# A fused attention and mixture-of-experts kernel: the tokens of experts three to eight turned by DMA transposes in place of TensorE transposes

## The chip, the cores and the metric

The kernel runs on one core of a Trainium2 chip. Its time is the device time of one execution in microseconds (us). The engines of a core work side by side, each in the order of its own queue: PE (TensorE, matmuls and transposes; PEld is its weight load), DVE (VectorE), ACT (ScalarE), POOL (GpSimd) and SP (SyncE, which here issues most DMAs). They wait for each other by semaphores.

## The reference

Attention over 8 batches of 12 heads, 448 positions and head size 64, with capped scores, is followed by a layer of eight experts to which tokens are given greedily.

```python
scores = cap * tanh(scale * q @ k.T / cap)
attn   = exp(scores - max); attn /= sum + 1e-9
x      = (attn @ v) as 3584 tokens x 768
logits = x @ w_gate                      # 8 experts, cap = 448 tokens each
for idx in argsort(-logits.flatten()):   # best (token, expert) pair first
    if token is free and expert has room: assign
for e in range(8):
    h = maximum(x[mask] @ w1[e], 0)      # 768 -> 1024
    out[mask] = h @ w2[e]                # 1024 -> 768
```

All is float32. Every expert gets exactly 448 tokens.

## The kernel before, in words

**Stages.** `attention` takes some 335 us and writes x (token by token) to a DRAM tensor `xs`. `ffn_all` first finishes what attention left over, with the search for the first expert's tokens between, and then runs the eight experts. The experts are found one after another: the search finds which expert fills first and which 448 tokens it gets, the FFN of that expert runs, and the search for the next one runs in the gaps.

**The order of the work.** In `ffn_all` PE, ACT, DVE and POOL run in the order in which the source writes their instructions (`manual_schedule`, L701). SP is not in that list; its DMAs are placed by the scheduler. The FFN is a sequence of matmuls; after each one `tick` (L806) counts up `now`. The search is a Python generator (`phases0`, L669, with `select`, `search` and `finalise`); every `yield n` means "go on n ticks later", and `step` (L690) then writes its next few instructions into the queues between two FFN matmuls. So the search's steps stand at fixed places between matmuls. In one step of `select` some compares are put on DVE (L503) and, for thresholds from the third on, on ACT (L500, `cmpA`); some ticks later PE adds their counts up (L507, `psR`), and DVE derives the next thresholds (L511, L515). The last step of `finalise` is a PE matmul (L644) and a DVE reduction (L648) that give `idx`, the token list. Then come the update of the search's tables (L651 on), 9 ticks, the proposals of the next search, 30 ticks, and `search`, whose first compares come 5 ticks later. For the eighth expert `last` (L590) stands in place of the search; it has no compares.

**One expert.** A period is 320 ticks. `ffn1` (L814) runs for f = 0 to 7: 18 matmuls each, 128 features of the 1024, for 448 tokens, as three products per slice of 128 of the 768 columns. `ffn2` (L846) runs for u = 0 to 7: four blocks of tokens (128, 128, 128, 64) times two halves of 384 output columns, 24 matmuls each, 16 for the last block. Float32 operands are cut into a rounded part and a rest ("h" and "l"), on ACT and on POOL for weights (`cut`, L752: `w1h`, `w1l`, `w2h`, `w2l`), on ACT and DVE for x (`cutx`, L800: `xgh`, `xgl`). PSUM tiles `psH` (three buffers) are emptied by ACT (L833, L861, L864).

**The tokens.** When `idx` is known, the next `tick` calls `gather` (L777): four indirect DMAs from POOL bring the 448 rows of 768 floats into the tile `xgp`, tokens on partitions, 128, 128, 128 and 64. The FFN needs x with columns on partitions. `xtr(p,c)` (L792) turns one slice of 128 columns: four PE transposes into a PSUM tile `psX`, then `cutx`. For experts three to eight, the list `CP` (L771) puts the six calls into `ffn2` of the expert before: u = 5 after matmuls 12 and 20, u = 6 after 4 and 20, u = 7 after 4 and 12. For the first two experts other lists say where, and these stay.

**The weights.** `load1` (L738) brings one eighth of w1 (384 KB), `load2` (L745) a quarter of w2 (768 KB), both from SP, with four buffers each. The source calls those of the next expert at u = 4 (w1 0 and 1), 5 (w1 2, w2 0), 6 (w1 3) and 7 (w2 1); SP can issue one as soon as it has read the expert's number and a buffer is free, since nothing ties it to PE's place.

Of the kernel before, what the change touches and what calls it, by code (L numbers as in the profile page):

```python
# [6 lines left out]
F32=mybir.dt.float32; F32R=mybir.dt.float32r; BF16=mybir.dt.bfloat16; F16=mybir.dt.float16; I32=mybir.dt.int32; I16=mybir.dt.int16  # L7
AF=mybir.ActivationFunctionType; ALU=mybir.AluOpType; AX=mybir.AxisListType
# [323 lines left out]
class Routing:  # L332
# [266 lines left out]
    def finalise(s,wp,L,update):  # L599
# [49 lines left out]
        s.results.append((idx,s.ei))  # L649
        yield 1  # L650
        if update:  # L651
          with s.tc.issue_after(mark.ins) if s.cur==0 else nullcontext():
            z=wp.tile([112,1],F32,name="zz")
            v.tensor_scalar(z,oi[:,0,0,0:1],0.0,None,op0=ALU.mult)
            v.scalar_tensor_tensor(gt,m[:,0,:],z,m[:,1,:],op0=ALU.add,op1=ALU.add)
            v.scalar_tensor_tensor(qq,pi,s.cap-0.5,gt,op0=ALU.is_lt,op1=ALU.mult)
            v.scalar_tensor_tensor(T["op"],qq,-2.0,T["op"],op0=ALU.mult,op1=ALU.add)
            ns=wp.tile([112,8],F32,name="ns"); pen=wp.tile([112,8],F32,name="pen")
            v.tensor_scalar(ns,s.e8c,s.e8s,z,op0=ALU.not_equal,op1=ALU.add)
            v.tensor_scalar(pen,ns,-0.5,2.0,op0=ALU.add,op1=ALU.mult)  # L660
            v.tensor_scalar(pen,pen,FMAX,None,op0=ALU.mult)
            v.tensor_tensor(s.e8m,s.e8m,ns,op=ALU.mult)
            v.tensor_tensor(L,L,pen.unsqueeze(1).broadcast_to([112,NC,8]),op=ALU.min)
            yield 9
# [15 lines left out]


W1B=4; W2B=4
def ffn_all(nc, tc, ctx, rt, xs, w1, w2, out, ident, E, wp, deferred, xctx, gen):
# [11 lines left out]
    def units(n):  # L695
        for _ in range(n):
            if deferred: late.append(deferred.pop(0)())
    def posts():
        while late: late.pop(0)()
    N0=1; UN=[1,2,1,2,0,2,2,1,2,2,0,2,2,2,0,0]  # L700
    ctx.enter_context(tc.manual_schedule(engines={ET.PE,ET.Activation,ET.DVE,ET.Pool}))  # L701
    with tc.issue_after(rt.mark[0].ins):
        units(1)
    posts()
    m=0
    wu=[None]; end=[-99]
# [31 lines left out]
    def load1(p,i,gate=None):  # L738
        if p>=E: return
        e=expert(p)  # L740
        t=ws.tile([128,DC,128],F32,name="w1r",bufs=W1B)
        if gate is not None: nc.gpsimd.tensor_copy(t[0:1,0,0:1],gate)
        nc.sync.dma_start(t,w1[bass.ds(e,1),:,i*128:i*128+128].rearrange("o (c p) f -> p (o c) f",p=128))
        raw[p,1,i]=t
# [23 lines left out]
        view=use=lambda t:t.rearrange("p (o d) -> p o d",o=2)  # L768
        cut((p,2,hf,i),src,[128,2*HD],"w2",8,None,view,use)
    xgs={}; xgT={}  # L770
    CP=[[int(y) if y!='-' else None for y in x] for x in ',,,,,-01,2-3,45'.split(',')]  # L771
    CL=[[]]*6+[[None,None,0],[1,2]]
    def newx(p):
        if p not in xgT: xgT[p]=(fp.tile([128,DC,C],F32R,name="xgh"),fp.tile([128,DC,C],F32R,name="xgl"))
# [2 lines left out]
    def gather(p):  # L777
        if p>=E or p in xgs: return
        need(p)
        t=xgs[p]=xgp  # L780
        for j,(o,n) in enumerate(TS):
            g=nc.gpsimd.indirect_dma_start(out=t[:n,j*DM:(j+1)*DM],out_offset=None,in_=xs,in_offset=bass.IndirectOffsetOnAxis(ap=res[p][0][:n,j:j+1],axis=0))  # L782
        return g
# [8 lines left out]
    def xtr(p,c):  # L792
        if p>=E or c is None: return
        newx(p)
        gather(p)
        ps=pt.tile([128,512],F32,name="psX")
        for j,(o,n) in enumerate(TS):
            nc.tensor.transpose(ps[:,o:o+128],xgs[p][:,j*DM+c*128:j*DM+c*128+128],ident)  # L798
        cutx(p,c,ps)
    def cutx(p,c,ps):  # L800
        h,l=xgT[p]
        src=ps[:,:C]
        nc.scalar.activation(h[:,c,:],src,AF.Copy)  # L803
        lo=nc.vector.tensor_tensor(l[:,c,:],src,h[:,c,:].bitcast(F32),op=ALU.subtract)
    pend=[]; cnt=[0]; cur=[0]; bc=[0]; BG=11
    def tick(n=1):  # L806
        cnt[0]+=n; bc[0]+=n; now[0]+=n
        if bc[0]>=BG:
            if pend: bc[0]=0; scatter(*pend.pop(0))
        if len(res)>cur[0]+1 and cur[0]+1 not in xgs: bc[0]=0; gather(cur[0]+1)  # L810
        if cnt[0]>=hint[0]:
            cnt[0]=0; step()
    hh={}
# [52 lines left out]
    need(0)  # L866
    WG=3; NW=12; WJ=4
    for i in range(WG): load1(0,i)
    mk=gather(0)
    with tc.issue_after(mk.ins):  # L870
        tok=xgp[0:1,2*DM:2*DM+1]
        for i in range(WG,W1B): load1(0,i,tok)
        load2(0,0,tok)
        load2(0,1,tok)
    warm(NW)
    step(); step()
    step()
# [5 lines left out]
    for p in range(E):  # L883
        lastp=p==E-1; cur[0]=p
        for f in range(FC):
            if f==0: load2(p,2)
            if f+W1B-1<FC and (p==0 or f+W1B-1>=W1B): load1(p,f+W1B-1) if (p,1,f+W1B-1) not in raw else None
            if f==2: load2(p,3)
            work={}
            if f+2<FC and (p,1,f+2) not in spl: work[3]=[lambda: split1(p,f+2)]  # L890
            at={0:[(11,0,0)],1:[(11,0,1)],2:[(11,0,2)],3:[(11,1,0)],4:[(11,0,3)],5:[(11,1,1)],6:[(11,1,2)],7:[(11,1,3)]}
            if p==0: at={1:[(11,0,0)],2:[(11,0,1)],3:[(11,0,2)],4:[(11,0,3)],5:[(11,1,0)],6:[(3,1,1),(11,1,2)],7:[(3,1,3)]}
            for n,hf,i in at.get(f,()): work[n]=[lambda hf=hf,i=i: split2(p,hf,i)]
            if p==1 and f==0: work[1]=[lambda: xtr(1,4)]; work[4]=[lambda: xtr(1,5)]
            ffn1(p,f,work)
        if lastp:
            while pend: scatter(*pend.pop(0))
            ih=f2.tile([128,2],I32,name="ih")
            for k in range(2): nc.gpsimd.tensor_scalar(ih[:,k:k+1],res[p][0][:,2:3],2.0,float(k),op0=ALU.mult,op1=ALU.add)
            nc.gpsimd.drain()  # L900
            lp[0]=False
            out2=out.rearrange("n (q d) -> (n q) d",q=2)
            for t,hf in [(t,hf) for t in (3,0,1,2) for hf in range(2)]:
                ffn2(p,t,hf,[])
                if t==2: put(out2,ih[:,hf:hf+1],ons[p][0][:,t*DM+hf*HD:t*DM+hf*HD+HD])
                elif hf==1: scatter(p,t)
            break
        for u in range(8):
            if u==4: load1(p+1,0); load1(p+1,1)
            if u==5: load1(p+1,2); load2(p+1,0)  # L910
            if u==6: load1(p+1,3)
            if u==7: load2(p+1,1)
            wk={5:{14:[lambda: split1(p+1,0)]},6:{8:[lambda: split1(p+1,1)]}}.get(u,{})
            if p<1 and u==7: wk={15:[lambda: xtr(1,3)]}
            ffn2(p,u%4,u//4,(CL if p<1 else CP)[u],wk)
            if u>3: pend.append((p,u%4))


def full(nc,tc,q,k,v,cap,wg,w1,w2,out):
    with ExitStack() as ctx:  # L920
# [2 lines left out]
        xs=dr.tile([3584,768],F32,name="xs")  # L923
        NDEF=4
        xd=dr.tile([2 if NDEF<4 else NDEF-2,128,6,448],F32,name="xd")
        ident=cp.tile([128,128],F32,name="ident"); make_identity(nc,ident)
        L1=cp.tile([112,32,8],F32,name="L1")
        r=Routing(nc,cp,3584,8); r.ident=ident; r.tc=tc
# [18 lines left out]
        ffn_all(nc,tc,ctx,r,xs,w1,w2,out,ident,8,wp,deferred,xctx,r.phases(wp,L1,turned))  # L947


_INS=["q","k","v","cap","moe_w_gate","moe_w1","moe_w2"]  # L950
# [24 lines left out]
```

## Time and profile before

| | |
|---|---|
| median of 3 runs | 906.31 us (905.91 to 907.29) |
| the profiled execution | 906.85 us, its span 905.1 us |
| mean granted PE clock | 0.995 |
| PE busy | 876.5 us, 97% of the span |
| PE transposes of `xtr` (L798) | 176, mean 272 ns |
| `gather` DMAs (L782) | 32, mean 1.07 us on POOL |
| DMA queue q1 (SP's DMAs) | 285104 packets, 99.70 MB |

The profile shows one execution. A timeline row gives the start in us from the span's start, the duration, the engine, the source line, the operation, the tile written and the tiles read, the shape, a count, and in brackets how long the engine sat idle before it and which instruction ended that. A row of groups gives busy us, mean ns, and idle time before. A row of a windows view gives, for a stretch of time, each engine's busy us, then the granted PE clock (1.00 is full), the share of the DMA engines and GB/s. Matmuls are pipelined: a row's duration overlaps the next one's start, so the distance of starts counts.

### The profile page before, as it was taken

How to read it: one execution, taken by the hardware profiler on the slowest of the kernel's cores; microseconds unless marked ns; L12 is line 12 of the kernel's file. 1: busy time of each engine (PE TensorE's matmuls, PEld its weight loads, DVE VectorE, ACT ScalarE, POOL GpSimd, SP SyncE). 2: the span in 40 equal slices, each digit the busy share in tenths (PEclk: the TensorE clock that was granted, in tenths of full speed). 3: DMA queues.
4: the chain of work that ended last, by engine and by line, in shares of the span. 5: the costliest groups of instructions: out<-in, count | busy, mean ns of one | idle time of the engine just before them, and what ended most of it. 6: DMA issues, size and time to landing. Idle time of an engine off the chain costs nothing.

```text
span 905.1 us, 17559 instructions
## 1 busy us (share of the span) xinstructions
PE 876.5 (97%) x6320; PEld 643.3 (71%) x6320; DVE 604.0 (67%) x2004; ACT 564.0 (62%) x844; POOL 349.9 (39%) x501
## 2 busy tenths in 40 slices
PE   6899999999999997799999999999999999999997
PEld 3333444444333345789989989989999999999997
DVE  3688988989888888766776776767767764231210
ACT  6998898889899948273582672762752752532521
POOL 8100000000000009482593492592682773754841
PEclk9999999999999999999999999999999999999999
DMA  8799999997994017741915616407407407416301
GB/s 117 113 136 140 128 171 173 139 164 120 198 175 72 1 58 246 248 157 45 313 45 171 196 36 226 157 19 236 150 18 253 149 3 251 149 55 236 112 10 53
DMA packets 291704, 123.09 MB, mean 136 GB/s; under 512 B 224768, under 2 KB 275712, under 8 KB 291104
## 3 DMA queue, kind: packets, MB, share of 16 engines
q1 hardware_dynamic: 285104, 99.70, 49.9%
q0 software_dynamic: 4656, 22.02, 6.8%
q8 instruction: 50, 0.82, 0.4%
q10 hardware_dynamic: 1856, 0.23, 0.2%
q14 instruction: 38, 0.31, 0.1%
HBM read 97.15 MB, written 24.77 MB: 135 GB/s over the span
## 4 chain that ended last, share of the span: by engine, by line
PE 72%; issue 12%; POOL 5%; DVE 5%; SPq 3%; DMA 1%; ACT 1%; POOLq 0%; ACTq 0%; DVEq 0%
PE psH L827 20%; PE psH L855 18%; PE psA L189 12%; PE psS L148 10%; PE psM L206 4%; SPq L92 2%; PE psS L153 2%; POOL w1l L759 2%; PE psX L798 2%; PE psM L37 1%; POOL out_dram L840 1%; POOL w2l L759 1%; DVE es L165 1%; POOL xg L782 1%; DVE cmpD L503 1%
## 5 line engine op out<-in xcount | busy, mean ns | idle before, releaser
L855 PE MATMUL psH<-w2h,hh 128*128 128x384 f32 x896 | 247.0, 342 | 0.0
L855 PE MATMUL psH<-w2l,hh 128*128 128x384 f32 x512 | 175.0, 342 | 0.0
L154 ACT ACTIVATE e<-psS 128x896 f32<-128x896 f32 x168 | 147.6, 909 | 31.3 <-PE psS L148 18.7
L855 PEld LDWEIGHTS psH<-w2h,hh 128*128 128x128 f32 x896 | 162.3, 189 | 0.2
L159 ACT ACTIVATE e<-e,bias 128x1792 f32<-128x1792 f32 (+2 forms) x74 | 147.3, 1991 | 2.0
L827 PE MATMUL psH<-xgh,w1h 128*128 128x448 f32 x384 | 143.4, 373 | 0.3 <-ACT xgh L803 0.3
L827 PE MATMUL psH<-xgh,w1l 128*128 128x448 f32 x384 | 141.6, 369 | 0.0
L827 PE MATMUL psH<-xgl,w1h 128*128 128x448 f32 x384 | 141.2, 368 | 0.0
L148 PE MATMUL psS<-tq,tk 64*64 64x448 f32 x1152 | 130.9, 548 | 7.4 <-DVE tq L133 3.4
L759 POOL TENSOR_TENSOR w1l<-w1r,w1h 128x768 fp32r<-128x768 f32 x62 | 114.2, 1843 | 28.6 <-ACT w1h L755 22.5
L189 PE MATMUL psA<-e,nv 64*64 64x448 f32 x1104 | 120.9, 541 | 1.2 <-DVE xT L199 1.2
L759 POOL TENSOR_TENSOR w2l<-w2r,w2h 128x768 fp32r<-128x768 f32 x64 | 118.1, 1846 | 9.0 <-ACT w2h L755 8.7
L459 POOL TENSOR_SCALAR r_Bt<-r_b 112x4 f16<-112x4 int32 x1 | 0.2, 199 | 303.7 <-DVE rin L243 303.7
L165 DVE TENSOR_TENSOR es<-es,e 64x896 f32<-64x896 f32 (+2 forms) x74 | 100.4, 1356 | 2.7 <-ACT e L159 1.3
L835 DVE SCALAR_TENSOR_TENSOR hh<-psH,hh 128x64 fp32r<-128x64 f32 (+1 forms) x128 | 44.1, 386 | 81.2 <-ACT hh L833 79.7
L861 ACT ACTIVATE on<-psH 128x384 f32<-128x384 f32 x48 | 23.6, 491 | 119.6 <-PE psH L855 119.6
L855 PEld LDWEIGHTS psH<-w2l,hh 128*128 128x128 f32 x512 | 96.5, 189 | 0.0
L148 PEld LDWEIGHTS psS<-tq,tk 64*64 64x64 f32 x1152 | 43.7, 133 | 73.9 <-issue 40.7
L189 PEld LDWEIGHTS psA<-e,nv 64*64 64x64 f32 x1104 | 46.5, 134 | 59.9 <-issue 50.5
L833 ACT ACTIVATE hh<-psH 128x448 fp32r<-128x448 f32 x64 | 34.8, 544 | 73.2 <-PE psH L827 61.1
L827 PEld LDWEIGHTS psH<-xgh,w1h 128*128 128x128 f32 x384 | 72.5, 189 | 5.9 <-ACT xgh L803 0.5
L827 PEld LDWEIGHTS psH<-xgh,w1l 128*128 128x128 f32 x384 | 72.3, 188 | 5.7
(334 smaller groups left out, 1320.6 us busy)
## 6 DMA issues: line engine op xcount, KB each, us to landing
w1r<-in_moe_w_dram SPq DMA_DIRECT2D x64, 384.0 KB, 3.9
w2r<-in_moe_w_dram SPq DMA_DIRECT2D x32, 768.0 KB, 8.0
k<-in_k_dram SPq DMA_DIRECT2D x92, 112.0 KB, 3.4
q<-in_q_dram SPq DMA_DIRECT2D x92, 112.0 KB, 4.0
nv<-in_v_dram SPq DMA_DIRECT2D x72, 128.0 KB, 3.9
xs<-xn SPq DMA_DIRECT2D x4, 1344.0 KB, 7.4
xs<-xn SPq DMA_DIRECT2D x4, 896.0 KB, 5.1
xd<-xT SPq DMA_DIRECT2D x2, 1344.0 KB, 7.0
```

What stands on the lines that cost most here:

```text
L148: for c in range(2): nc.tensor.matmul(ps[c*64:c*64+64,h,:S],tks[g,0][hp,o,u*128+c*64:u*128+c*64+64],tks[g,1][hp,o,:],start=True,stop=True)
L154: nc.scalar.activation(ev(g,r),ps[:,:,:S],AF.Tanh,scale=sr[0])
L159: act=lambda: nc.scalar.activation(e,e,AF.Exp,scale=sr[1],bias=bias)
L165: t=es_t[g]; add=lambda o,a,b: nc.vector.tensor_tensor(o,a,b,op=ALU.add)
L189: nc.tensor.matmul(avp[g,o][h*64:h*64+64,:S],lhs,rhs[hp,h,:],start=(j==0 and x==0),stop=j==3)
L206: nc.tensor.matmul(ps[g*32:g*32+32,:S],lhs,rhs,start=first,stop=last)
L759: (eng or nc.gpsimd).tensor_tensor(view(l),r,view(h).bitcast(F32),op=ALU.subtract)
L827: nc.tensor.matmul(ps[:,:C],a[:,c,:],b[:,c,:],start=(m==0),stop=(m==DC*3-1)); m+=1
L833: nc.scalar.activation(h[:,:C],ps[:,:C],AF.Relu)
L835: nc.vector.scalar_tensor_tensor(h[:,d:d+b-a],ps[:,a:b],0.0,h[:,a:b].bitcast(F32),op0=ALU.max,op1=ALU.subtract)
L855: nc.tensor.matmul(ps[:,:HD],h[:,f,a:a+128],spl[p,2,hf,f//2][w][:,f%2,:],start=(m==0),stop=(m==nm-1))
L861: if t<3: nc.scalar.activation(ons[p][0][:,t*DM+hf*HD:t*DM+hf*HD+HD],ps[:,:HD],AF.Copy)
```

## The change

For experts three to eight (`p` of 2 to 7) the 24 PE transposes and the six `cutx` of each go. In their place:

- `tick`, right after `gather(n)`, calls the loads of w1 0 and 1, and sets four calls of `planes` 14, 22, 30 and 38 ticks later.
- `planes(p,j)`: one ACT copy takes the j-th piece of the gathered tokens as 16-bit integers and writes the two halves of each float32 apart (tile `pl`, two buffers, 2 x 768 16-bit values a token). An SP DMA stores it to the DRAM scratch `xz`, 896 rows of 768 16-bit values, two rows a token. After the fourth, two SP DMA transposes read `xz`, 896 x 384 values each, and write `xgp` with columns on partitions; the halves land side by side, so the result is float32 again.
- `cutt(p,c0,c1)` cuts two slices of columns at once, from SBUF: ACT copy to `xgh`, DVE subtraction to `xgl`, 896 elements each. It is called in `ffn2` of the expert before, at u = 6 after matmul 20 and at u = 7 after matmuls 6 and 13.

SP joins the engines that run in the source's order, and three `issue_after` blocks go.

```diff
         if update:
-          with s.tc.issue_after(mark.ins) if s.cur==0 else nullcontext():
+          if True:
...
-    ctx.enter_context(tc.manual_schedule(engines={ET.PE,ET.Activation,ET.DVE,ET.Pool}))
-    with tc.issue_after(rt.mark[0].ins):
-        units(1)
+    ctx.enter_context(tc.manual_schedule(engines={ET.PE,ET.Activation,ET.DVE,ET.Pool,ET.SP}))
+    units(1)
...
-    CP=[[int(y) if y!='-' else None for y in x] for x in ',,,,,-01,2-3,45'.split(',')]
...
+    TD=14; TJ=8; xq=[]
+    def planes(p,j):
+        o,n=TS[j]
+        pl=fp.tile([128,2,DM],I16,name="pl",bufs=2)
+        nc.scalar.activation(pl[:n].rearrange("p h d -> p d h"),xgs[p][:n,j*DM:(j+1)*DM].bitcast(I16).rearrange("p (d h) -> p d h",h=2),AF.Copy)
+        nc.sync.dma_start(xz[2*o:2*o+2*n].rearrange("(p h) d -> p h d",h=2),pl[:n])
+        if j==3:
+            for a in (0,3): nc.sync.dma_start_transpose(xgp[:,a*C:a*C+3*C].bitcast(I16).rearrange("p (c t) -> p c t",c=3),xz[:,a*128:a*128+384])
+    def cutt(p,c0,c1):
+        newx(p)
+        h,l=xgT[p]
+        x=xgp[:,c0*C:c1*C].rearrange("p (c t) -> p c t",c=c1-c0)
+        nc.scalar.activation(h[:,c0:c1,:],x,AF.Copy)
+        nc.vector.tensor_tensor(l[:,c0:c1,:],x,h[:,c0:c1,:].bitcast(F32),op=ALU.subtract)
...
-        if len(res)>cur[0]+1 and cur[0]+1 not in xgs: bc[0]=0; gather(cur[0]+1)
+        if len(res)>cur[0]+1 and cur[0]+1 not in xgs:
+            bc[0]=0; n=cur[0]+1; gather(n)
+            if n>1:
+                load1(n,0); load1(n,1)
+                xq.extend((now[0]+TD+TJ*j,lambda j=j: planes(n,j)) for j in range(4))
+        while xq and xq[0][0]<=now[0]: xq.pop(0)[1]()
...
-    mk=gather(0)
-    with tc.issue_after(mk.ins):
-        tok=xgp[0:1,2*DM:2*DM+1]
-        for i in range(WG,W1B): load1(0,i,tok)
-        load2(0,0,tok)
-        load2(0,1,tok)
+    gather(0)
+    tok=xgp[0:1,2*DM:2*DM+1]
+    for i in range(WG,W1B): load1(0,i,tok)
+    load2(0,0,tok)
+    load2(0,1,tok)
...
-            if u==4: load1(p+1,0); load1(p+1,1)
+            if u==4 and p<1: load1(p+1,0); load1(p+1,1)
...
-            ffn2(p,u%4,u//4,(CL if p<1 else CP)[u],wk)
+            if p and not lastp:
+                for m,c in {6:[(20,0)],7:[(6,2),(13,4)]}.get(u,()): wk[m]=wk.get(m,[])+[lambda c=c: cutt(p+1,c,c+2)]
+            ffn2(p,u%4,u//4,CL[u] if p<1 else [],wk)
...
+        xz=dr.tile([896,768],I16,name="xz")
```

More of the change, by code (lines that the diff above doesn't have):

```diff
@@ L682, with ffn_all @@
 W1B=4; W2B=4
-def ffn_all(nc, tc, ctx, rt, xs, w1, w2, out, ident, E, wp, deferred, xctx, gen):
+def ffn_all(nc, tc, ctx, rt, xs, xz, w1, w2, out, ident, E, wp, deferred, xctx, gen):
     C=448; DM=768; DC=6; DF=1024; FC=8; HD=384
@@ L946, in full @@
         deferred=[lambda f=f: f((px,xr)) for f in deferred]
-        ffn_all(nc,tc,ctx,r,xs,w1,w2,out,ident,8,wp,deferred,xctx,r.phases(wp,L1,turned))
+        ffn_all(nc,tc,ctx,r,xs,xz,w1,w2,out,ident,8,wp,deferred,xctx,r.phases(wp,L1,turned))
 _INS=["q","k","v","cap","moe_w_gate","moe_w1","moe_w2"]
```

## The prediction

> **What bounds the kernel now.** I read the page's busy shares first, then the windows by stage, then the timeline of each engine around the changed place.
>
> ```profile
> span 905.1 us, 17559 instructions
> PE 876.5 (97%) x6320; PEld 643.3 (71%) x6320; DVE 604.0 (67%) x2004; ACT 564.0 (62%) x844; POOL 349.9 (39%) x501
> ...
> 582.00:647.31 65.31, 65.31 (x372) 60.34 (x372) 46.72 (x227) 34.82 (x80) 38.16 (x41) 1.00 0.43 139
> ```
>
> The last row is one expert's period (us, then busy time of PE, weight loads, DVE, ACT, POOL; clock; DMA share; GB/s). PE is busy for 65.31 of 65.31 us at full clock, so in this stage every PE instruction added or removed counts, and so does every wait that PE does not have today. ACT is idle half the time, but its idle half is not free: it works in order, and PE waits for some of its results at fixed places.
>
> **The transposes that go.** From the timeline of PE, a group of four transposes between two matmuls:
>
> ```profile
> 636.18 0.52 PE L855 MATMUL psH<-w2h,hh 128*128 128x384 f32 x2
> 636.54 0.60 PE L798 MATMUL psX<-ident,xg 128*128 128x128 f32 x4
> 636.89 0.42 PE L855 MATMUL psH<-w2l,hh 128*128 128x384 f32 x1
> ```
>
> The group pushes the next matmul back by 636.89 - 636.54 = 0.35 us; the rest of its 0.60 us overlaps its neighbours. Six groups an expert, 2.1 us, and six experts: 36 x 0.35 = **-12.6 us**. The 36 pairs of ACT copy and DVE subtraction that go with them leave engines on which PE does not wait today, so they give nothing more.
>
> **The edits of order.** The three blocks that go name a PE, a DVE and a POOL instruction, and those engines already run in written order. SP's issues before are these:
>
> ```profile
> 614.71 1.63 SPq L743 DMA_DIRECT2D w1r<-in_moe_w_dram  x3
> 616.53 0.73 SPq L750 DMA_DIRECT2D w2r<-in_moe_w_dram  x1
> 617.51 0.37 SPq L743 DMA_DIRECT2D w1r<-in_moe_w_dram  x1
> 618.13 1.62 SPq L750 DMA_DIRECT2D w2r<-in_moe_w_dram  x2
> ```
>
> That is w1 0, 1, 2, w2 0, w1 3, w2 1, w2 2: the source's order already. These edits cost nothing, from the first experts too. What does move SP is the new work in its queue: behind the first two w1 loads now come four stores that wait for ACT, and two transposes that wait for all stores; only then the five other loads.
>
> **What ACT must now do, and when.** Rows around one gather (the start of the fifth expert's), from the timelines of PE, POOL and ACT:
>
> ```profile
> 619.02 0.19 PE L644 MATMUL psR<-ev,r_sel 128*128 128x28 f16 x1
> 628.90 0.18 PE L507 MATMUL psR<-r_cd,r_bo 128*128 128x4 bf16 x1
> ...
> 619.93 0.98 POOL L782 DMA_INDIRECT xg<-xs,idx  x1 [8.55 <-DVE zz L654]
> 621.22 1.20 POOL L782 DMA_INDIRECT xg<-xs,idx  x1 [0.30 <-issue]
> 622.72 1.05 POOL L782 DMA_INDIRECT xg<-xs,idx  x1 [0.30 <-issue]
> 624.07 1.13 POOL L782 DMA_INDIRECT xg<-xs,idx  x1 [0.30 <-issue]
> ...
> 625.08 0.49 ACT L861 ACTIVATE on<-psH 128x384 f32<-128x384 f32 x1 [3.67 <-PE psH L855]
> 626.90 0.51 ACT L500 ACTIVATE cmpA<-r_VAt,r_T8A 128x252 bf16<-128x252 f16 x1 [1.33 <-DVE r_VAt L482]
> 627.31 0.19 ACT L500 ACTIVATION_READ_ACCUMULATOR cmpA<-r_VAt,r_T8A 128x1 bf16 x1
> ```
>
> L644 gives the expert's token list. By the yields in the source (1, 9, 30, 5 ticks, a tick being one FFN matmul) the next search's first compare is put on ACT 45 ticks after it, and PE's L507, which adds up its counts, 55 ticks after: 628.90. The four planes are put on ACT 15, 23, 31 and 39 ticks after it, so **all four stand ahead of that compare in ACT's queue**, with the L861 eviction between the third and the fourth. If they are late, the compare is late, and PE waits at L507.
>
> Prices, from these rows:
>
> ```profile
> DMA to landing us min/median/max: 4.4/4.4/4.6
> DMA to landing us min/median/max: 7.3/8.6/9.2
> ...
> L833 ACT ACTIVATE hh<-psH 128x448 fp32r<-128x448 f32 x64 | 34.8, 544 | 73.2 <-PE psH L827 61.1 <-PE psR L507 8.1 <-issue 3.6
> L154 ACT ACTIVATE e<-psS 128x896 f32<-128x896 f32 x168 | 147.6, 909 | 31.3 <-PE psS L148 18.7 <-PE psS L153 11.9
> L159 ACT ACTIVATE e<-e,bias 128x1792 f32<-128x1792 f32 (+2 forms) x74 | 147.3, 1991 | 2.0
> ...
> DMA to landing us min/median/max: 3.3/3.5/7.5
> xs<-xn SPq DMA_DIRECT2D x4, 448.0 KB, 4.3
> ```
>
> - Gather, from issue to landing (least, middle, most): the first row is three pieces of the first expert's gather, the second this expert's, beside some 3 MB of weight loads. After the change the five loads come later and the gather is nearly alone: 4.4 us, bounds 4.4 and 8.6. The first piece lands at 624.4, the second at 625.7.
> - A plane: 1536 elements. From 448 to 896 elements ACT took 365 ns more, 0.81 ns each, so 909 + 640 x 0.81 = 1.43 us; by the 1792 row in proportion 1.71. I take 1.45, being a plain copy like the first two.
> - Its store, 384 KB: that expert's w1 loads of 384 KB landed in 3.3 to 7.5 us, 3.5 in the middle, a 448 KB store in 4.3. I take 3.5. The plane tile has two buffers, so **the third plane must wait until the first one's store has landed**, and the fourth for the second's.
>
> The chain: plane 1 624.4 to 625.9, its store landed 629.4; plane 2 to 627.4, landed 630.9; plane 3 629.4 to 630.9; eviction to 631.35; plane 4 to 632.8; compare and read-out (0.70) to 633.5; L507 at 633.6 and not 628.90: a wait of **4.7 us**. Lower bound, no wait for stores: 624.4 + 4 x 1.43 + 0.49 + 0.70 = 631.3, a wait of 2.4. Upper, with 8.6, 1.71 and 4.3: pieces land at 627.2, 629.8 and later, plane 3 starts at 633.2, plane 4 ends at 637.2, a wait of 9.1. Nothing covers it: PE runs in order, and FFN matmuls stand behind L507. The late eviction itself costs nothing, since psH has three buffers and PE stands at L507 before it wants that one again. It happens where a search follows the gather: experts three to six, for the search of expert eight has no compares. 4 x 4.7 = **+18.8 us** (9.6 to 36.4).
>
> **The clock after such a wait.** The one long PE gap of this stage before the change:
>
> ```profile
> 375.45 0.27 PE L477 MATMUL psR<-r_id,r_VA 112*128 112x112 f16 x2 [2.56 <-DVE r_VA L452]
> 376.96:380.34 3.38, 3.38 (x18) 3.38 (x18) 1.77 (x3) 0.00 (x0) 0.91 (x3) 0.50 0.29 91
> ```
>
> After 2.56 us idle the granted clock was 0.50 for 3.38 us: 1.7 us of PE's time gone. A wait of 4.7 us should do the same: 4 x 1.7 = **+6.8 us** (0, if it doesn't, to twice that).
>
> **The transposes' own time.** Rows: 1344 KB moved plainly, and what a packet costs.
>
> ```profile
> xTr<-xd SPq DMA_DIRECT2D x2, 1344.0 KB, 7.4
> q1 hardware_dynamic: 285104, 99.70, 49.9%
> ...
> 749.74 0.19 PE L644 MATMUL psR<-ev,r_sel 128*128 128x28 f16 x1
> 776.34 0.36 PE L827 MATMUL psH<-xgh,w1h 128*128 128x448 f32 x1
> 776.54 0.37 PE L827 MATMUL psH<-xgl,w1h 128*128 128x448 f32 x1
> L165 DVE TENSOR_TENSOR es<-e,e 128x1792 f32<-128x1792 f32 (+1 forms) x24 | 46.8, 1951 | 8.8 <-ACT e L159 8.8
> ```
>
> No transposing DMA is in the trace. A packet took 0.499 x 905.1 x 16 / 285104 = 25.3 ns of one engine. The two transposes move 896 rows x 768 two-byte values; a row's 128 columns are 256 B, so 5376 pieces, 5376 x 25.3 / 16 = 8.5 us. A plain copy of the size gives 7.4. If the pieces were 32 B, 43,008 of them would take 68 us. I take 8.5, the nearer of the two ends, since 256 B is the unit that the access pattern itself names, and keep 7.4 and 68.
>
> Experts seven and eight have no L507 to wait for, so PE comes on time. L644 at 749.74 is 130.72 after the 619.02 above; the fourth plane ends at 632.8 + 130.7 = 763.5, its store (192 KB, 3.5) lands at 767.0, the transposes at 775.5. Then 896 elements on ACT (0.91) and on DVE (1951 / 2 = 0.98): columns 2 and 3 are cut at 777.4. PE reaches the FFN at 776.34 - 2.1 = 774.25 and wants the low part of column 2 seven matmuls of 0.20 later, 775.65: a wait of 1.75, twice, **+3.5 us**. For experts three to six the wait and the slow clock have moved PE 6.4 us back, and 6.4 - 1.75 = 4.65 us are to spare: nothing.
>
> [...]
>
> **The five loads** then follow the transposes. Before, everything from 614.71 to the last w2 load's landing,
>
> ```profile
> 619.11 0.64 SPq L750 DMA_DIRECT2D w2r<-in_moe_w_dram  x1
> w2r<-in_moe_w_dram SPq DMA_DIRECT2D x1, 768.0 KB, 14.6
> L759 POOL TENSOR_TENSOR w1l<-w1r,w1h 128x768 fp32r<-128x768 f32 x62 | 114.2, 1843 | 28.6 <-ACT w1h L755 22.5
> ```
>
> was 5.2 MB in 19.0 us, 3.6 us per MB. So after 775.5 the third w1 tile lands at 776.9 (its split stands at about 776.5) and the first w2 at 779.7 (about 778). One or two us late, and the split's product is wanted 33 matmuls (6.6 us) after its place, less 0.8 (768 elements on ACT) and 1.84 (POOL): 3.9 us of cover. Nothing; if the transposes took 3 us more, this would begin to show.
>
> **Sum:** -12.6 + 18.8 + 6.8 + 3.5 = +16.5. The profiled execution took 906.85 us (its span of 905.1 and 1.75 around it), so 923.3; the median of the runs, 906.31, is 0.54 below it: **922.8 us**.
>
> **Rivals.**
>
> 1. *The wait is short, and the kernel faster.* If the plane stores come back before ACT wants the buffers, only the copies' own time is left: 2.4 us four times, with gaps just under the 2.56 us after which the clock was seen to drop. Then -12.6 + 9.6 = -3.0, 903 us; with no wait at all 893.7. For it: 4.4 us gathers, with little else on the DMA engines. Against: a store landing within 2 us of its issue, where nothing of this size in the trace took less than 3.3. It decides from where the compare is done before 632.1, that is 3.2 us a time without the clock's loss, 1.5 with it.
>
> 2. *The transposing DMAs are slow.* At twice the 8.5 us, experts seven and eight wait 8.5 us more each and the four others 8.5 - 4.65: another 2 x 8.5 + 4 x 3.85 = 32, 955 us. At 68 us the same sum gives 2 x 59.5 + 4 x 54.85 = 338, about 1260. For it: the unit in which a transposed row is written is unknown here, and small packets are dear in this trace. Against: only pieces below 256 B make it so, and q1, half idle over the span, has room. [...]
>
> 3. *The wait is there but the clock holds:* 922.8 - 6.8 = 916.0; it lies in my own range.
>
> 4. *The stalls cancel the gain* (all waits together within 12.6 +- 1.8 us): no change.
>
> **How the numbers follow.** A change of less than 0.2% (1.8 us) is no change for this kernel. The forecast with rival 3: 0.49, its own range 912 to 936. Rival 1: 0.27, 893 to 904. Rival 4: 0.06. Rival 2: 0.18, from 936 up. The range 897 to 940, whose top is transposes of some 14 us, leaves out the best part of rival 1 (0.06) and most of rival 2 (0.14). Faster 0.27, same 0.06, slower 0.67.
>
> **What will show it.** In the timeline of the changed kernel: L644 to the first L507 after it, 9.88 us before, should be near 14.6 for experts three to six; the first compare should come right behind the fourth plane; the third plane should end ACT's wait on a store's DMA; the windows should show clock 0.50 for some 3 us after each such wait. PE's period should be 2.1 us shorter and the waits longer. The first matmul of experts seven and eight should wait for the cut at most 2 to 3 us. The prediction is wrong if L507 stands within 12.5 us of L644, or if the transposes land more than 12 us after their issue.

## The result, and the profile after

The changed kernel takes **1043.15 us** (median of 4 runs, 1041.22 to 1045.31) beside 906.11 us of the kernel before: a ratio of **1.151**, 95% interval 1.148 to 1.154. The prediction said slower, and 922.8 us, with a range from 897 to 940. The sign was right, and the size far off. Times are medians; one execution of the later kernel with 46 ticks took 1074.06 us at a granted clock of 0.752 and is left out of that kernel's time.

The page of the changed kernel (busy us and share, then groups: busy us, mean ns, and idle time of that engine ahead of them):

```profile
span 1043.5 us, 17357 instructions
PE 877.1 (84%) x6176; PEld 641.6 (61%) x6176; DVE 602.2 (58%) x1986; ACT 724.7 (69%) x850; POOL 350.4 (34%) x501
...
L802 ACT ACTIVATE pl<-xg 128x1536 int16<-128x1536 int16 (+1 forms) x24 | 166.7, 7197 | 16.5 <-DMA xg<-xs,idx 16.5
```

The span grew by 138.4 us. ACT gained 160.7 us of busy time, and 166.7 of it is one group: the 24 plane copies `pl`, at **7.2 us each**. The prediction had 1.45. PE has 144 instructions fewer and the same busy time, and is idle far more. What it waits for, first in the kernel after (us in total, times, longest):

```profile
PE psR L507 <- ACT cmpA L500: 69.5, 3, 23.7
PE psR L507 <- DVE cmpD L503: 33.3, 18, 24.6
PE psH L872 <- ACT on L878: 26.6, 2, 13.5
PE psH L844 <- ACT xgh L810: 5.7, 2, 3.0
PE psH L872 <- DVE on L882: 4.3, 2, 2.2
```

and the same view of the kernel before:

```profile
PE psR L507 <- DVE cmpD L503: 5.5, 13, 0.7
```

So L507 costs 69.5 + 33.3 - 5.5 = 97.3 us more, the second FFN matmul (L872) 30.9, the cut columns (L844) 5.7, and 2.0 more in waits for DVE's half of them, 7.7. The rows around the fifth expert's gather, the stretch that the prediction worked through (timelines of PE and ACT):

```profile
667.13 0.19 PE L644 MATMUL psR<-ev,r_sel 128*128 128x28 f16 x1
700.18 0.16 PE L507 MATMUL psR<-r_cd,r_bo 128*128 128x4 bf16 x1 [23.02 <-ACT cmpA L500]
...
671.96 20.71 ACT L802 ACTIVATE pl<-xg 128x1536 int16<-128x1536 int16 x3 [2.44 <-DMA xg<-xs,idx]
692.16 0.83 ACT L878 ACTIVATE on<-psH 128x384 f32<-128x384 f32 x1
692.87 6.97 ACT L802 ACTIVATE pl<-xg 64x1536 int16<-64x1536 int16 x1
699.32 0.72 ACT L500 ACTIVATE cmpA<-r_VAt,r_T8A 128x252 bf16<-128x252 f16 x1
```

L644 to L507 is 33.05 us; it was 9.88 before, and 14.6 by the prediction. The order is the one foretold: three planes, the eviction, the fourth plane, and right behind it the compare that PE waits for. Only the copies are five times as long, so ACT is held for 27.4 us without a gap. They also hide what the prediction saw as the second link: no plane waits for a store any more. ACT's waits at L802 are all for gathered pieces (16.5 us); the first store is issued at 679.15, and the third plane, the next in its buffer, begins some 6.6 us later.

The clock after this wait (a window of 3.38 us from L507 on: us, then busy time of PE, weight loads, DVE, ACT, POOL; clock; DMA share; GB/s):

```profile
700.18:703.56 3.38, 3.38 (x15) 3.38 (x15) 2.69 (x15) 1.66 (x5) 0.00 (x0) 0.50 0.28 61
703.56:708.00 4.44, 4.44 (x23) 4.29 (x22) 2.21 (x14) 1.77 (x6) 1.03 (x2) 0.81 1.07 132
```

Over the span the mean granted clock is 0.934, against 0.995 before.

At experts seven and eight, where no L507 waits, PE ran into its accumulators instead. Rows of PE, ACT and SP for expert seven:

```profile
872.31 1.01 PE L872 MATMUL psH<-w2h,hh 128*128 128x384 f32 x2 [13.53 <-ACT on L878]
...
851.12 20.82 ACT L802 ACTIVATE pl<-xg 128x1536 int16<-128x1536 int16 x3 [2.90 <-DMA xg<-xs,idx]
...
882.08 7.62 SPq L805 DMA_TRANSPOSE xg<-xz  x2
...
889.61 0.95 ACT L810 ACTIVATE xgh<-xg 128x896 fp32r<-128x896 f32 x1 [7.45 <-DMA xg<-xz]
892.00 1.79 ACT L810 ACTIVATE xgh<-xg 128x896 fp32r<-128x896 f32 x2 [1.06 <-DMA xg<-xz]
```

The eviction L878 that PE waits for stands behind three planes, from 851.12 to 871.43; all three `psH` are full, and PE waits 13.53 us. The two transposes, issued from 882.08 on, have landed by 889.6 and 892.0.

### The profile page after: what moved, and what is told of

Its sections match the earlier page's. It is cut to its first block, busy times and chain, and to the rows that moved or that the text cites. A ratio compares the mean times of both kernels' runs of the same rounds, so it can differ in the third digit from the quotient of the medians.

```text
span 1043.5 us, 17357 instructions
## 1 busy us (share of the span) xinstructions
PE 877.1 (84%) x6176; PEld 641.6 (61%) x6176; DVE 602.2 (58%) x1986; ACT 724.7 (69%) x850; POOL 350.4 (34%) x501
## 4 chain that ended last, share of the span: by engine, by line
PE 53%; issue 14%; ACT 12%; DVE 7%; DMA 6%; POOL 4%; SPq 3%; POOLq 0%; DVEq 0%; ACTq 0%
PE psH L844 15%; PE psA L189 10%; PE psH L872 10%; ACT pl L802 9%; PE psS L148 9%; PE psM L206 3%; DMA xg<-xs,idx 2%; DMA w1r<-in_moe_w_dram 2%; DVE cmpD L503 2%; SPq L92 1%; PE psS L153 1%; DVE es L165 1%; POOL w1l L758 1%; PE psM L37 1%; POOL w2l L758 1%
## 5 line engine op out<-in xcount | busy, mean ns | idle before, releaser
L872 PE MATMUL psH<-w2h,hh 128*128 128x384 f32 x896 | 253.4, 352 | 30.9 <-ACT on L878 26.6
L872 PEld LDWEIGHTS psH<-w2h,hh 128*128 128x128 f32 x896 | 169.8, 197 | 32.4 <-ACT on L878 27.3
L872 PE MATMUL psH<-w2l,hh 128*128 128x384 f32 x512 | 178.3, 348 | 0.0
L802 ACT ACTIVATE pl<-xg 128x1536 int16<-128x1536 int16 (+1 forms) x24 | 166.7, 7197 | 16.5 <-DMA xg<-xs,idx 16.5
L154 ACT ACTIVATE e<-psS 128x896 f32<-128x896 f32 x168 | 147.4, 909 | 30.9 <-PE psS L148 18.3
L844 PE MATMUL psH<-xgh,w1h 128*128 128x448 f32 x384 | 145.2, 378 | 6.0 <-ACT xgh L810 5.7
L844 PE MATMUL psH<-xgl,w1h 128*128 128x448 f32 x384 | 142.9, 373 | 2.0 <-DVE xgl L811 2.0
L844 PE MATMUL psH<-xgh,w1l 128*128 128x448 f32 x384 | 142.9, 372 | 0.0
L857 POOL DMA_INDIRECT out_dram<-on,idx x31 | 31.2, 1007 | 260.1 <-ACT on L878 190.2
L882 DVE TENSOR_TENSOR on<-psH,y 64x384 f32<-64x384 f32 x16 | 8.7, 546 | 164.9 <-ACT y L881 164.9
L872 PEld LDWEIGHTS psH<-w2l,hh 128*128 128x128 f32 x512 | 100.2, 196 | 0.0
L878 ACT ACTIVATE on<-psH 128x384 f32<-128x384 f32 x48 | 25.5, 532 | 100.9 <-PE psH L872 100.7
L507 PE MATMUL psR<-r_cd,r_bo 128*128 128x4 bf16 x52 | 9.2, 177 | 99.5 <-ACT cmpA L500 69.5
```

The lines of the kernel that those rows point to most:

```text
L154: nc.scalar.activation(ev(g,r),ps[:,:,:S],AF.Tanh,scale=sr[0])
L802: nc.scalar.activation(pl[:n].rearrange("p h d -> p d h"),xgs[p][:n,j*DM:(j+1)*DM].bitcast(I16).rearrange("p (d h) -> p d h",h=2),AF.Copy)
L844: nc.tensor.matmul(ps[:,:C],a[:,c,:],b[:,c,:],start=(m==0),stop=(m==DC*3-1)); m+=1
L857: st=nc.gpsimd.indirect_dma_start(out=dst,out_offset=bass.IndirectOffsetOnAxis(ap=ix,axis=0),in_=src,in_offset=None)
L872: nc.tensor.matmul(ps[:,:HD],h[:,f,a:a+128],spl[p,2,hf,f//2][w][:,f%2,:],start=(m==0),stop=(m==nm-1))
```

## The experiments

All ratios are to the kernel before. Where a kernel's lines are one further down, its L803, L811, L812, L845, L873, L879, L882 and L883 are L802, L810, L811, L844, L872, L878, L881 and L882 of the changed kernel.

### The turning left out

```diff
-                xq.extend((now[0]+TD+TJ*j,lambda j=j: planes(n,j)) for j in range(4))
+                pass
```

> The changed kernel without planes, stores and DMA transposes: the 24 PE transposes of experts three to eight are gone and nothing turns the tokens; they are cut as they were gathered. It leaves out the turning. By the prediction's first step the time falls by 12.6 us, to 893.5 us. If PE waits somewhere for the cut or for the loads that now come in the source's order, it falls by less.

Measured: 893.08 us, ratio 0.986 (0.984 to 0.988). The 144 PE transposes were worth 13.2 us against the predicted 12.6. All of the 150 us between this kernel and the changed one come from the planes, their stores and the transposing DMAs, and from what waits for them. PE's busy time here is 858.9 us, with the same 6176 instructions as after; its waits at L507 are 8.7 us in all. From the page:

```profile
span 891.0 us, 17258 instructions
PE 858.9 (96%) x6176; PEld 627.0 (70%) x6176; DVE 605.4 (68%) x1986; ACT 560.3 (63%) x826; POOL 348.0 (39%) x501
```

### The edits of order alone

Of the change, only SP in written order and the three `issue_after` blocks gone.

> The kernel before with the edits of order alone: SP in the source's order and the three issue_after blocks gone. The prediction says nothing changes: 906.1 us within 0.2%. If the order of SP's DMAs mattered, it moves by more.

Measured: 906.56 us, ratio 1.0004 (0.9994 to 1.0013). These edits cost nothing.

### The copies and the transposes by themselves

Behind the last expert of the kernel before, each form of the copy twice on a 128 x 1536 tile of 16-bit values, on three engines, then the four stores and two transposes, of 896 x 384 and of 256 x 768 values (extra work, so the kernel's time isn't compared). "Jumping" writes value after value to alternate halves of the tile, as the change does; "stepping" reads every second value and writes side by side, or, as a write (L930), reads straight and writes every second value. The comments at the ends of the lines are not in the kernel.

```diff
+        nc.scalar.activation(par(qb),seq(qa),AF.Copy)     # L927 jumping write
+        nc.scalar.activation(pln(qb),zip2(qa),AF.Copy)    # L928 stepping read
+        nc.scalar.activation(qb,qa,AF.Copy)               # L929 straight
+        nc.scalar.activation(zip2(qb),pln(qa),AF.Copy)    # L930 stepping write
+        nc.scalar.activation(par(fb),seq(fa),AF.Copy)     # L931 float32, jumping write
+        nc.scalar.activation(fb,fa,AF.Copy)               # L932 float32, straight
+        nc.vector.tensor_copy(par(qb),seq(qa))            # L933 to L935: the first three on DVE
...
+        nc.gpsimd.tensor_copy(par(qb),seq(qa))            # L936 to L938: on POOL
```

> The kernel before, and behind its end copies and transposes by themselves; they work on zeros and change no output. ACT copies of 128 x 1536 16-bit values: jumping write, stepping read, straight, and a write that steps by two values; 128 x 768 float32 values: jumping write and straight; the first three on DVE and on POOL too. Then an 896 x 384 DMA transpose and one of 256 x 768, each alone. Theory 1 (jumping write): only the first kind is slow on ACT, 7 us, the float32 one in proportion to its 768 values, 3.5 us; the stepping write too if it is a matter of single 16-bit writes. Theory 2 (the type): all 16-bit copies on ACT take 7 us and the float32 ones 0.8. Theory 3: both stepping kinds are slow. The transpose alone should land 6 to 8 us after its issue if what the changed kernel shows is its own time, and clearly sooner if it was the queue.

The timeline of that tail (start, us):

```profile
899.20 6.96 ACT L927 ACTIVATE qb<-qa 128x1536 int16<-128x1536 int16 x1
906.18 1.48 ACT L928 ACTIVATE qb<-qa 128x1536 int16<-128x1536 int16 x1
907.70 1.48 ACT L929 ACTIVATE qb<-qa 128x1536 int16<-128x1536 int16 x1
909.21 1.91 ACT L930 ACTIVATE qb<-qa 128x1536 int16<-128x1536 int16 x1
911.15 1.53 ACT L931 ACTIVATE qb<-qa 128x768 f32<-128x768 f32 x1
912.72 0.84 ACT L932 ACTIVATE qb<-qa 128x768 f32<-128x768 f32 x1
913.59 4.02 DVE L933 COPY qb<-qa 128x1536 int16<-128x1536 int16 x1 [37.87 <-ACT qb L932]
...
918.64 0.56 DVE L935 COPY qb<-qa 128x1536 int16<-128x1536 int16 x1
919.33 6.94 POOL L936 COPY qb<-qa 128x1536 int16<-128x1536 int16 x1 [18.80 <-DVE qb L935]
...
964.92 3.07 SPq L944 DMA_TRANSPOSE xg<-xz  x1
970.11 0.15 DVE L945 COPY xg<-xg 128x1 f32<-128x1 f32 x1 [20.74 <-DMA xg<-xz]
```

The same 1536 values take ACT 6.96 us with the jumping write and 1.48 with the stepping read, and a straight copy takes 1.48 too. So the price hangs on the **write**, not on the number of values, and neither the 16-bit type by itself nor a read that steps costs it. Single 16-bit writes are not the reason either: with a step of two values they take 1.91. It is the far jump, and the type counts with it: 768 float32 values with the same jump take 1.53 against 0.84, not the 3.5 expected. That is 0.9 ns more a value, where a 16-bit value pays 3.6 ns more. A read that jumps as far was not tried. DVE and POOL pay as well (4.02 against 0.56, 6.94 against 1.47). One transpose of 896 x 384 values has landed 970.11 - 964.92 = 5.2 us after its issue began, 3.07 of it issuing on SP. That is sooner than the 6 to 8 us expected if the 7.5 us of the changed kernel's first transpose were all its own; what the rest is isn't shown.

### The copy turned round

```diff
-        nc.scalar.activation(pl[:n].rearrange("p h d -> p d h"),xgs[p][:n,j*DM:(j+1)*DM].bitcast(I16).rearrange("p (d h) -> p d h",h=2),AF.Copy)
+        nc.scalar.activation(pl[:n],xgs[p][:n,j*DM:(j+1)*DM].bitcast(I16).rearrange("p (d h) -> p h d",h=2),AF.Copy)
```

> The changed kernel with one edit: the plane copy runs over the same 1536 values, first all low halves and then all high halves, so that ACT writes them side by side and it is the read that steps over every second value. Same result. Theory 1 (the 7 us of a plane copy come from the write, which jumps between two planes 1536 bytes apart at each value): a copy takes about 1.45 us, PE waits at the search's first count 4 to 5 us after four gathers, some 1 to 3 us at the FFN of the last two experts, and the time is 915 to 930 us. Theory 2 (16-bit integers are slow on ACT, whatever the order): 7 us again, 1043 us. Theory 3 (any step of two values on either side costs): 2 to 5 us a copy, 950 to 1020 us.

Measured: **924.87 us**, ratio 1.021 (1.019 to 1.023). The order in which one copy walks its values is worth 118 us. What is left is the kernel that the prediction priced, and its number, 922.8, is 2.1 us off (which of its terms hold, and which only cancel, is said below). Rows of PE and ACT at the fifth expert's gather, and the window behind L507:

```profile
628.33 0.19 PE L644 MATMUL psR<-ev,r_sel 128*128 128x28 f16 x1
642.30 0.16 PE L507 MATMUL psR<-r_cd,r_bo 128*128 128x4 bf16 x1 [3.94 <-ACT cmpA L500]
...
638.53 1.48 ACT L802 ACTIVATE pl<-xg 128x1536 int16<-128x1536 int16 x1 [1.88 <-DMA xz<-pl]
...
642.30:645.68 3.38, 3.38 (x15) 3.38 (x15) 2.69 (x15) 1.66 (x5) 0.00 (x0) 0.50 0.28 61
```

L644 to L507 is 13.97 (predicted 14.6), the wait 3.94 (4.7), the third plane waits for a store's DMA as foretold, and the clock is 0.50 for the foretold 3.38 us.

### Four buffers of their own

To the turned copy, three planes in one tile that shares the space of `xgl`, the fourth in its own, so that no plane waits for a store.

```diff
+        if j==0: pw[0]=fp.tile([128,3,2,DM],I16,name="pl",tag="xgl")
+        pl=pw[0][:,j] if j<3 else fp.tile([128,2,DM],I16,name="pl3",bufs=2)
```

> The side-by-side copy, and the planes in four buffers of their own (three lie in the space of xgl, which is free then), so that no plane waits for a store. Same result. The prediction's chain said that the store's wait makes 2.3 of its 4.7 us. In the run with the side-by-side copy the gathered pieces landed nearly 2 us apart, so I now expect the fourth plane only about 1 us earlier, PE's wait at the search's first count 2.9 us in place of 3.9, and 918 to 921 us. If stores were the larger part, 912 to 916; if they don't matter, 924.9.

Measured: 914.16 us, ratio 1.009 (1.007 to 1.012), 4 to 7 us better than expected and inside the 912 to 916 that stood for the stores being the larger part. The store's wait is gone; the wait at L507 shrinks to 2.2 to 3.1 us a time, near the prediction's lower bound of 2.4, which has no wait for stores. It is not the planes' own time alone: ACT still stands idle 0.2 to 1.0 us ahead of some second, third and fourth planes for a gathered piece.

### The search later

To the turned copy with two buffers: the next search 24 ticks later.

```diff
-                yield 30
+                yield 54 if 2<p<s.E-1 else 30
```

> The side-by-side copy, and the search behind the gathers of experts three to six begins 24 ticks later (54 in place of 30), so that its first compares stand behind the planes with time to spare. Same result. Theory 1 (the wait at that count, with the slow clock after it, is what is left of the loss, 6 to 7 us four times): those waits go, the transposes come 1 to 3 us late for every expert, as they do for the last two, and the time is 903 to 908 us. Theory 2 (the transposes bind anyway, the wait at the count only hid it): 915 to 925 us.

Measured: 916.73 us, ratio 1.011 (1.009 to 1.013): not the 903 to 908 of the theory that the four planes ahead of the compare are all there is to it. L507 still waited, now for DVE's compares (2.31 us at 572.37, 1.29 at 638.57). The time lies in the range of theory 2, but the columns are only a part of it: PE waits 5.2 us for them, 16.2 at L507 (8.7 without any turning), and is busy 869.1 us, 10.2 above the kernel without turning.

### The planes on POOL

To the four buffers, the copies moved off ACT:

```diff
-        nc.scalar.activation(pl[:n],xgs[p][:n,j*DM:(j+1)*DM].bitcast(I16).rearrange("p (d h) -> p h d",h=2),AF.Copy)
+        nc.gpsimd.tensor_copy(pl[:n],xgs[p][:n,j*DM:(j+1)*DM].bitcast(I16).rearrange("p (d h) -> p h d",h=2))
```

> The side-by-side copy by POOL in place of ACT, planes in four buffers of their own. POOL has nothing to do between the gather and the next scatter, and a copy took 1.47 us there by itself. Same result. Nothing then stands before the search's compares on ACT. Theory 1: no wait at the count, the transposes start about 1.5 us sooner than with the side-by-side copy on ACT, and are still about 1 us late for six experts: 896 to 902 us, faster than before. Theory 2 (the transposes bind): 905 us or more.

Measured: 921.60 us, ratio 1.017 (1.015 to 1.019): a miss, worse than on ACT. Rows of POOL, DVE and PE:

```profile
562.94 6.17 POOL L803 COPY pl<-xg 128x1536 int16<-128x1536 int16 x4
...
562.37 3.49 DVE L460 TENSOR_SCALAR r_Ct<-r_c 112x32 f16<-112x32 int32 x1
566.11 1.68 DVE L462 TENSOR_TENSOR r_VC<-r_P,r_Ct 112x256 f16<-112x256 f16 x1
...
570.47 0.18 PE L507 MATMUL psR<-r_cd,r_bo 128*128 128x4 bf16 x1 [3.71 <-DVE cmpD L503]
```

L460 takes 3.49 us here and L462 1.68; with the planes on ACT they took 0.17 and 0.42 (in the run with the search later). During POOL's four copies DVE gets little done, so the last steps of the search's proposal, and behind them the compares, come some 5 us late (L482 runs at 569.18, PE's turn for it at 563.80). The wait at L507 has only changed its owner. The rows look as if DVE stood still for whole copies: L460 ends at 565.86, about where POOL's second copy does (the four take 6.17 us from 562.94 on). What holds DVE up isn't shown.

### The same with transposes by token pieces

To the planes on POOL: pieces gathered into buffers of their own, and four transposes by pieces of tokens. Each waits for its own piece's store alone, but in SP's queue the first two stand behind the issue of the next piece's store, and the last two come together.

```diff
+        for i in {1:(0,),2:(1,),3:(2,3)}.get(j,()):
+            a,k=TS[i]
+            nc.sync.dma_start_transpose(xgp[:,:DC*C].bitcast(I16).rearrange("p (c t) -> p c t",c=DC)[:,:,2*a:2*a+2*k],xz[2*a:2*a+2*k,:])
```

> As the one with POOL's planes, and a DMA transpose for each of the four pieces, issued as soon as that piece's store has landed, in place of two that wait for all. The gather goes into the space of xgh and the transposes write xgp, so nothing is overwritten too early. Same result. The last piece is 128 rows, so the tokens should be there some 4 us sooner: theory 1 gives the time of the kernel that turns nothing, 893 to 896 us. Theory 2 (SP's issue of a transpose, about 1.4 us a piece and in a row with the stores, eats it up): as with POOL's planes, 896 to 902 us.

Measured: 921.46 us, ratio 1.017 (1.015 to 1.019): a miss for the same reason. L507 waits 24.4 us in all for DVE, as with two transposes (24.7), where the kernel without turning has 8.7.

### Buffers of their own and a later search together

On ACT, four buffers, and 46 or 42 ticks for 30; then 46 with the transposes by pieces.

```diff
-                yield 30
+                yield 46 if 2<p<s.E-1 else 30
```

> The two changes that each helped alone, together: planes by stepping read on ACT in four buffers of their own (run with own buffers: 914.16 us), and the next search 16 ticks later (46 for 30), which is 3.2 us. In the run with own buffers PE stood 10.5 us at L507 in all, 2.2 to 2.6 us a time, and its busy time in the last two thirds was 8.0 us above that of the kernel without the turning (451.2 against 443.2), which is the clock. Theory 1: the last plane ends at most 2.6 us too late and nothing else is behind the wait; 3.2 us more room takes away the waits and the clock's loss: 914.2 - 10.5 - 8.0 = 895.7, between 893 and 900. Theory 2: a search put later meets other work ahead of its compares (DVE's addition L882 that waits for ACT's eviction), as with 24 ticks and two buffers: waits of 1 to 2.5 us stay, 905 to 912.

> As the run before it, with the search 12 ticks (2.4 us) later. Theory 1: of the waits of 2.2 to 2.6 us at most 0.2 us a time stay, too short for the clock to drop: 895 to 900. Theory 2: 905 to 912 again; if the two runs differ by more than 4 us, the place of the search among the evictions decides, not its distance.

> ACT planes in own buffers, search 16 ticks later, and the transposes cut by token pieces (three, each issued once its pieces are stored) in place of two by columns. Theory 1: the first matmuls of experts seven and eight waited 0.7 us each for the cut columns; with earlier transposes these waits go, nothing else: 1.3 us below the run with 16 ticks and two transposes, 892 to 899. Rival: three transposes whose rows are split cost more of SP and of the DMA engines, and the weight loads behind them come late: slower than that run, by 2 to 10 us.

Measured: 910.56 (ratio 1.006, 1.004 to 1.008) with 46, 916.68 (1.011, 1.009 to 1.013) with 42, 911.10 (1.005, 1.004 to 1.007) with 46 and pieces. Theory 2 holds for 46; 42 lies above its range too, and is no better than 30 (914.16, the intervals overlap). The pieces, four transposes here too, bring nothing that can be measured, and don't harm either. Rows of ACT, DVE and PE of the run with 46:

```profile
567.65 1.49 ACT L803 ACTIVATE pl<-xg 64x1536 int16<-64x1536 int16 x1
569.16 0.49 ACT L882 ACTIVATE y<-psH 64x384 f32<-64x384 f32 x1
...
569.68 0.55 DVE L883 TENSOR_TENSOR on<-psH,y 64x384 f32<-64x384 f32 x1 [6.07 <-ACT y L882]
570.15 0.37 DVE L482 CAST r_VAt<-psR 128x224 f16<-128x224 f32 x1
...
571.44 0.18 PE L507 MATMUL psR<-r_cd,r_bo 128*128 128x4 bf16 x1 [1.74 <-DVE cmpD L503]
```

The fourth plane makes the eviction L882 late, DVE's addition L883 waits 6.07 us for it, and the search's first step L482 stands behind that addition in DVE's queue, at 570.15. With 42 ticks it stands there too (L883 waits 5.70 us, L482 runs at 568.90); with 30 it ran ahead of the addition. So the place among the evictions says why 12 ticks more than 30 gained nothing, but not why 42 and 46 differ by 6 us. Of the 8.1 us between their profiled spans some 3.2 are waits at L507 (20.5 against 17.3). Most of the rest is PE's granted clock: among the experts it falls once with 46 (behind a wait of 2.49 us at 518.94) and three times with 42 (behind 2.06 us at 570.19, behind 2.34 at 639.37, and behind 1.00 and 0.66 close together at 788 to 789), and each time some 1.7 us of PE's time are gone.

### The search 30 ticks later

```diff
-                yield 30
+                yield 60 if 2<p<s.E-1 else 30
```

> Four buffers of their own and the search 30 ticks (6 us) later. In the run with 16 ticks DVE's addition L883 stood ahead of the search's first steps in DVE's queue and waited 6.07 us for ACT's L882, which came behind the fourth plane; DVE was free of it at 570.2, and the search's turn by PE stood at 566.75. Theory: 14 ticks more put the search behind that addition, and PE's waits at the first L507 of a search (5.9 us in all there) go with 2 to 4 us of clock: 911.4 - 5.9 - 3 = 902, between 899 and 906; the waits at the later L507 (5.9 in all, 3.3 of them also without any turning) stay. Rival: some other eviction's addition stands ahead of the search there too, or the search ends too late for the next token list: 908 to 918.

Measured: 907.98 us, ratio 1.0015 (0.9999 to 1.0031), short of the expected 902 and a tie with the kernel before. Waits of PE:

```profile
PE psR L507 <- DVE cmpD L503: 11.8, 18, 1.4
PE psH L845 <- DVE xgl L812: 3.9, 6, 0.7
...
PE psH L845 <- ACT xgh L811: 3.2, 5, 1.7
```

The waits at the first L507 have gone as expected, but for one of 0.86 us (17.3 us at L507 in all with 46 ticks, 11.8 here, 8.7 without any turning), and the clock is back at 0.997. But now PE reaches the next FFN in time, and waits for the columns: 7.1 us over all experts, where the 46-tick run had 0.8 + 1.7. With the waits, 893.08 + 7.1 + (11.8 - 8.7) = 903.3, and PE's busy time is 3.2 us above that of the kernel without turning (862.1 against 858.9): 906.5, which leaves 1.5 us without an owner. From 440 us on the difference is 3.5 us (446.7 against 443.2) for the same 2436 matmuls; what makes it isn't shown. No version tried that turns the tokens beats the kernel before; this one ties with it.

## Why the prediction was right or wrong

**The step that failed is a price:** "A plane: 1536 elements ... 1.43 us; by the 1792 row in proportion 1.71. I take 1.45, being a plain copy like the first two." It measured 7.2, over four times the upper bound. The rows it was worked out from, L833 and L154, write their values side by side; the plane copy writes each value 1536 bytes away from the one before. The bounds were drawn from two rows that share the property which the new operation lacks, and so both ends missed it. Put into the prediction's own chain, 6.97 a plane gives 624.4 + 4 x 6.97 + 0.49 + 0.70 = 653.5, and L507 24.6 us late; it waited 22.8 to 24.6. The mechanism was right, and the kernel with the copy turned round, to which 1.45 does apply (1.48), takes 924.87 against the 922.8 forecast. That the two are so near is in part luck. Against the kernel without turning, the four long waits at L507 there make 16.7 us for the 18.8 foretold, the slow clock behind them 8.9 for 6.8 (from the granted clock over the 6.76 us behind each), the columns 3.2 for 3.5, and a late weight split 1.0 for nothing: errors of up to 2.1 us that partly cancel.

The prediction named two signs of being wrong. L507 within 12.5 us of L644 did not come up, nor did transposes that land more than 12 us after their issue (9.9); none of the signs was for a dearer copy. The measured time lies in the stretch that the prediction left to rival 2, slow transposes, but not for that rival's reason.

What the runs show of a plane's price lies on the side of the write: 1.48 us side by side, 6.96 when each 16-bit value goes 1536 bytes from the one before. It is not one price per jump, since a float32 value that jumps as far pays 0.9 ns more, a quarter of the 3.6 of a 16-bit one. Why is not shown.

**The transposes gone**, -12.6: right, 13.2.

**The edits of order**, 0: right, 1.0004 with 1 inside its interval.

**The place of the wait** (all four planes ahead of the compare, PE at L507, four times): right, four waits of 22.8 to 24.6 us. The third plane's wait on a store shows only with the short copy (1.88 us).

**"The late eviction itself costs nothing"**: right with short copies, wrong with the long ones. It rested on PE standing at L507 before it wants `psH` again. At experts seven and eight there is no L507, and PE waited 13.5 and 2.2 us at each, 30.9 in all.

**The clock**, 1.7 us a wait and 6.8 in all: a wait's price is right at the least, 0.50 for 3.38 us behind it, but there are six long waits and not four, and behind the one shown the next 4.4 us run at 0.81. It was taken from one wait of 2.56 us at L477, and there it was luck: the same wait in the changed kernel (2.57 us at 374.98) left the clock at 1.00. PE's busy time, for the same matmuls, is 877.1 - 858.9 = 18.2 us above the kernel without turning.

**The transposes' own time**, 8.5 us from 25.3 ns a packet: near. The first landed 7.5 us after the first issue, the second 9.9, and one alone takes 5.2. Rival 2 falls. One alone moves 688 KB in its 5.2 us, 132 GB/s from issue to landing, with 3.07 us of SP's issue in it. What the transfer alone runs at isn't shown.

**Experts seven and eight**, +3.5 for the cut columns: 7.7 was waited there. The last run showed the other half of that step: once no L507 holds PE up, the same lateness costs at the other experts too: 7.1 us over six experts.

**The five loads**, 0: nearly right. In the changed kernel no split makes PE wait; in the kernel with the copy turned round PE waits once, 0.97 us at 810.46 for a split of expert seven's w1, whose load came late.

The account is best drawn up against the kernel without turning, whose span is 152.5 us shorter (1043.5 - 891.0): 102.8 - 8.7 = 94.1 at L507, 30.9 at L872, 7.7 at the columns and 18.2 of clock make 150.9. The 1.6 us between are not settled. From the kernel before, it is 14.1 us less (905.1 - 891.0) by the transposes: 138.4.

The rivals: the first (short wait, faster) was tried by buffers and by a later search. With short waits alone it gave 903 us, on the ground that gaps just under 2.56 us leave the clock alone; four buffers gave waits of 2.19 to 3.10 us, but the clock fell behind the shortest of them too (to 0.63), and the time was 914.16. No run that turns the tokens came under the kernel before, since after each wait that was taken away another one stood: the store, the planes themselves, DVE's delay beside POOL's copies, the addition behind a late eviction, at last the columns. 893 us, the kernel without any turning, stays a bound that none of these reached.

## What to carry to other kernels

Price a copy by how it walks memory, here on the side it **writes** (6.96 us jumping, 1.48 straight; a read that jumps far was not tried), and not by its number of values alone; a new access pattern needs bounds from rows that have it, or an upper bound several times the straight one (4.7 times here). Where a copy must deinterleave, let the read step and the write run (1.48 us on ACT here). And work moved off a full engine goes into another engine's ordered queue: before counting the gain, list what stands behind it there, and who waits for that, one link further than the first.

## What the runs showed of the hardware

- Writes of 16-bit values that jump between two rows 1536 bytes apart: ACT 6.96 us against 1.48 straight for 128 x 1536, POOL 6.94 against 1.47, DVE 4.02 against 0.56. Reads that step by two values cost ACT and POOL nothing (1.48, 1.46) and DVE 0.40 more (0.96). A write that steps by two values took ACT 1.91. Float32 values that jump, 128 x 768 on ACT: 1.53 against 0.84.
- POOL's copies of 16-bit values held DVE up: 3.49 us for an operation of 0.17, 1.68 for one of 0.42. POOL's subtractions of the weight split (1.84 us each) run beside DVE's compares in the kernel before and in the changed one, and the compares keep their 0.44 us; whether POOL's operation or DVE's makes the difference wasn't tried.
- PE's clock fell after some waits shorter than 2.56 us, but not after all: over the next 3.38 us it was 0.63 behind one of 2.06 us and one of 2.19, 0.59 behind 2.31, 0.55 behind 2.58, yet it stayed at 1.00 behind one of 2.22 and one of 2.62, and behind single ones of 1.75, 1.74, 1.51 and 1.29. It also fell behind two short waits close together: with 42 ticks, behind waits of 1.00 and 0.66 us that end at 787.92 and 789.04 us, matmuls of 128 x 448 start 0.37 us apart in place of 0.20. Length alone doesn't decide: the same wait of 2.56 or 2.57 us at L477, some 375 us into these kernels, left the clock at 1.00 over the next 3.38 us in the changed kernel, and at 0.72 in the kernel before. By the 0.50 for 3.38 us that the window of the kernel before shows, an estimate is that up to 1.7 us of a difference in PE's busy time between two profiles can be this one wait. What else decides isn't shown.
